# One scale in place of five for the value matrices of five batches, and a new order table

## The chip, the cores and the metric

The kernel runs on one core of a Trainium2 chip. The metric is the device time of one execution in microseconds (us). The names used are those of the profile: PE is the matmul engine and PEld its weight loads, DVE, ACT and POOL are the vector, scalar and GpSimd engines, SP is the engine that issues nearly all DMAs (SPq its queue).

## The reference

Attention for 8 batches of 8 heads (sequence 576, head size 64) with a bias that depends on positions alone, then a gated layer on the heads put side by side (512 columns).

```python
scores = scale * np.matmul(q, k.transpose(0, 1, 3, 2))
...
scores = scores + bias.transpose(2, 0, 1)[None, :, :, :]
scores = scores - np.max(scores, axis=-1, keepdims=True)
attn = np.exp(scores)
attn = attn / (np.sum(attn, axis=-1, keepdims=True) + 1e-09)
return np.matmul(attn, v).astype(np.float32)
...
for k in range(K):
    gate_pre += conv_w[k][None, None, :] * xp[:, k:k + S, :]
gate = 1.0 / (1.0 + np.exp(-gate_pre))
val = x @ w_val
return (gate * val @ w_out).astype(np.float32)
```

## The kernel before

The work is cut into 32 pairs of heads (`order`: first batches 0 and 1, then batch after batch from 2 to 7, four pairs each, numbered 0 to 31) and 8 gated layers (`mlp`). A pair computes four blocks of 128 query rows, and every second pair a shared fifth block with the last 64 rows of two pairs. Per block: PE multiplies q and k into the PSUM tile `t_sp` (L702), DVE adds the bias and finds the row's extreme (`logits`, L748), ACT takes the exponential (`expo`, L760).

`TRANS` then has two ways. In the way "T" (pairs 0 to 5, 24 and 25) PE transposes the weights in fp32 (L891). In the way "D" (the other 24 pairs) ACT, DVE or POOL rounds the exponentials to fp16 (`top`, L195), POOL or DVE forms the rest (`rest`, L218), and a DMA on SP's queue transposes both parts (`swap`, L925 and L928). For the product with the values (`piece`, L958) the values of a D pair are split in two fp16 parts as well. That split is what the change is about:

- `ldv` (L630, L618 in the way T) loads a pair's values, 128 x 640 numbers, into `raw`, a buffer of the ring `w` that has 13; `vmax` (L633) finds the greatest magnitude of each partition on DVE and puts it in `vcol`.
- `vp_mm` (L636) transposes that column on PE, `vp_max` (L640) takes the greatest of all on DVE, `vscale` (L644) makes the pair's scale of it, `vinv` (L650) the inverse. These four steps run for each D pair.
- `vhi` (L654, ACT) writes the first fp16 part with the inverse as factor, `vlo` (L657, DVE) the second; from here on `piece` may run.
- PE's product is brought to SBUF (`t_xp`, the gated layer's input) by ACT with the pair's scale as factor (`ev`, `evr`, L213) and multiplied with the softmax' inverse sums by DVE (`mu`, L1014).

A batch has a scale of its own for the gated layer's input (`batch_scale`): `vb_max` (L570), `vb_mm` (PE, L573), `vb_all` (L576), `vb_scale`, `vb_inv` (L582). It is used much later, when ACT and DVE split `t_xp` in two fp16 parts: `split_hi` (L213, out `xh`), `split_lo` (L206, out `xl`). On POOL `split_lo` takes four instructions by way of `gtmp`. The gate is a convolution on `t_xp` (`taps`, L1151) and a Tanh on ACT (`sig`, L1164).

No queue decides the order at run time. `ORDER` is a packed table: for each place the number of a task and the engine that it goes to, of those that the task allows. Each engine runs its instructions in that order, and an instruction that has to wait holds up all behind it on its engine. A ring's buffer goes to its next taker in the table's order.

## Time and profile before

| | us |
|---|---|
| three runs, median (lowest to highest) | 663.69 (659.8 to 665.06) |
| profiled execution, its own time | 663.0 |
| its span, first to last instruction | 661.2 |
| PE, DVE, ACT, POOL busy in the span | 626.6, 596.0, 573.5, 489.2 |
| granted TensorE clock, mean | 0.988 |

The span is 1.8 us shorter than the execution's own time, which is 0.7 us under the median of the three runs. A busy time counts an instruction from its start to its end; on one engine the start of the next often lies before the end of the one ahead, and the profile's sums leave out what overlaps.

### The profile page before, as it was taken

The page shows a single profiled execution, that of the slowest core. Times are in us where ns is not written, and L with a number is a line of the kernel's source. Part 1 is how long each engine was busy: PE and PEld are TensorE (multiplying, and loading weights), DVE is VectorE, ACT ScalarE, POOL GpSimd, SP SyncE. Part 2 cuts the span into 40 slices and gives each one's busy share as a digit, 9 for nine tenths or more (in the row PEclk, how much of TensorE's full clock was granted, in tenths as well). Part 3 has the DMA queues.
Part 4 walks back from the last instruction along what each step waited for, and adds up shares of the span by engine and source line. Part 5 has one row for each costly group of instructions (what it writes and reads, how often), then busy time and mean ns, then how long its engine had stood idle before and what let it go on. Part 6 is the DMA issues. An engine that isn't in the chain of part 4 may idle for free.

```text
span 661.2 us, 16769 instructions
## 1 busy us (share of the span) xinstructions
PE 626.6 (95%) x6176; PEld 405.1 (61%) x6176; DVE 596.0 (90%) x1604; ACT 573.5 (87%) x1268; POOL 489.2 (74%) x539
## 2 busy tenths in 40 slices
PE   6869999999799999999998999999999999999997
PEld 2213667766466677657665576666676765767663
DVE  7999999999999799899998888998988889989982
ACT  6989999999899999889787999889889878989671
POOL 5576739676699898897788788887868868776430
PEclk9969999999999999999999999999999999999999
DMA  5879966336999999999999999999984998999622
GB/s 178 270 254 326 333 242 182 103 140 145 170 209 190 207 218 211 234 192 216 204 209 234 212 208 206 224 184 208 217 179 120 161 210 178 219 196 162 120 80 95
DMA packets 279106, 129.76 MB, mean 196 GB/s; under 512 B 255600, under 2 KB 255856, under 8 KB 279024
## 3 DMA queue, kind: packets, MB, share of 16 engines
q1 hardware_dynamic: 278880, 128.40, 89.5%
q8 instruction: 48, 0.79, 0.5%
q14 instruction: 34, 0.28, 0.2%
q10 hardware_dynamic: 144, 0.29, 0.1%
HBM read 44.64 MB, written 20.33 MB: 98 GB/s over the span
## 4 chain that ended last, share of the span: by engine, by line
PE 52%; DVE 13%; DMA 13%; POOL 9%; ACT 9%; issue 3%; SPq 1%; DVEq 0%; POOLq 0%; ACTq 0%
PE t_sp L702 12%; DMA t_pt<-t_d 12%; PE t_ps L958 10%; PE t_ps L1285 8%; PE t_ps L1219 7%; POOL t_d L218 6%; PE t_ps L891 5%; DVE t_d L748 4%; PE t_ps L337 4%; ACT t_d L760 3%; ACT t_d L195 2%; PE t_sp L718 2%; DVE rel L318 2%; PE t_ps L1004 1%; PE t_ps L1028 1%
## 5 line engine op out<-in xcount | busy, mean ns | idle before, releaser
L218 POOL TENSOR_TENSOR t_d<-t_d,t_d 128x128 f16<-128x128 f32 (+1 forms) x180 | 244.3, 1376 | 50.9 <-ACT t_d L195 46.5
L760 ACT ACTIVATE t_d<-t_d,nm 128x576 f32<-128x576 f32 x288 | 221.5, 771 | 24.3 <-DVE nm L748 23.6
L748 DVE CUSTOM_DVE_ANT_0 t_d<-t_sp,bias 128x576 f32<-128x576 f32 x256 | 186.4, 750 | 22.8 <-PE t_sp L702 16.4
L702 PE MATMUL t_sp<-t_qk 64*128 64x288 f32 x1024 | 170.0, 431 | 4.8 <-DVE nm L748 3.7
L958 PE MATMUL t_ps<-t_pt,t_w 128*64 128x256 f16 (+1 forms) x1664 | 122.6, 296 | 7.3 <-DMA t_pt<-t_d 4.1
L702 PEld LDWEIGHTS t_sp<-t_qk 64*128 64x128 f32 x1024 | 96.1, 187 | 52.6 <-DVE nm L748 16.2
L195 ACT CAST t_d<-t_d 128x576 f16<-128x576 f32 x155 | 99.6, 666 | 12.2 <-DMA t_pt<-t_d 7.6
L1219 PEld LDWEIGHTS <-wv 128*128 128x128 f16 x768 | 72.6, 98 | 29.6 <-issue 10.3
L958 PEld LDWEIGHTS <-t_w 128*64 128x64 f16 x1344 | 70.3, 110 | 24.6 <-issue 15.6
L1219 PE MATMUL t_ps<-xh,wv 128*128 128x256 f16 (+1 forms) x480 | 68.3, 286 | 0.0
L1151 DVE SCALAR_TENSOR_TENSOR t_ps<-t_xp,convw,t_ps 128x288 f32<-128x288 f32 x126 | 64.5, 516 | 1.6 <-ACT t_ps L1142 0.4
L1285 PE MATMUL t_ps<-wo,gh 128*128 128x512 f16 x240 | 57.8, 380 | 0.0
L760 ACT ACTIVATION_READ_ACCUMULATOR t_d<-t_d,nm 128x1 f32 x288 | 54.9, 191 | 0.0
L337 PE MATMUL t_ps<-rel,w 128*32 128x280 f32 (+17 forms) x352 | 44.5, 555 | 9.6 <-ACT t_be L356 4.4
L318 POOL TENSOR_SCALAR rel<-gt,sct,nb 128x560 f32<-128x560 f32 (+11 forms) x16 | 37.4, 2341 | 18.1 <-PE t_ps L337 17.8
L810 POOL TENSOR_SCALAR t_d<-t_d,rinv 128x576 f32<-128x576 f32 x56 | 41.9, 761 | 8.6 <-DVE rinv L790 7.6
L318 DVE TENSOR_SCALAR rel<-gt,sct,nb 128x576 f32<-128x576 f32 (+17 forms) x92 | 46.9, 570 | 1.2 <-PE t_ps L337 1.0
L891 PE MATMUL t_ps<-ident,t_d 128*128 128x128 f32 x324 | 43.4, 278 | 1.9 <-POOL t_d L810 0.8
L891 PEld LDWEIGHTS t_ps<-ident,t_d 128*128 128x128 f32 x324 | 35.3, 140 | 14.1 <-issue 4.4
L199 POOL TENSOR_SCALAR t_d<-t_d 128x576 f16<-128x576 f32 x47 | 34.0, 727 | 12.8 <-ACT t_d L760 10.5
L1285 PEld LDWEIGHTS <-gh 128*128 128x128 f16 x240 | 22.3, 99 | 27.4 <-issue 6.0
L195 ACT COPY t_pt<-t_ps 128x512 f32<-128x512 f32 (+1 forms) x82 | 36.2, 489 | 3.2 <-PE t_ps L891 2.8
(149 smaller groups left out, 1081.8 us busy)
## 6 DMA issues: line engine op xcount, KB each, us to landing
t_qk<-qkd SPq DMA_DIRECT2D x32, 576.0 KB, 4.7
bias_d<-t_be SPq DMA_DIRECT2D x36, 295.5 KB, 4.2
bias<-bias_d SPq DMA_DIRECT2D x16, 576.0 KB, 7.2
out<-t_w SPq DMA_DIRECT2D x32, 256.0 KB, 2.6
t_w<-vd SPq DMA_DIRECT2D x24, 320.0 KB, 3.7
t_w<-vn SPq DMA_DIRECT2D x8, 320.0 KB, 4.4
t_d<-wvd SPq DMA_DIRECT2D x4, 512.0 KB, 4.9
t_d<-wod SPq DMA_DIRECT2D x4, 512.0 KB, 4.1
```

Source lines behind the costliest of these rows:

```text
L195: A.copy(out=out, in_=in_)
L218: (V if e == "V" else G).tensor_tensor(out=out, in0=in0, in1=in1, op=ALU.subtract)
L318: (G if e == "G" else V).tensor_scalar(out=rel[g].t[:, 0:w], in0=src, scalar1=sct[:, mm : mm + 1], scalar2=nb1, op0=ALU.mult, op1=ALU.max,)
L337: T.matmul(pb[32 * g : 32 * g + 32, 0 : y - x], lhsT=w28, rhs=rel[g].t[:, x:y], start=True, stop=True, tile_position=(0, 32 * g),)
L702: T.matmul(ts[a][:, j, 0:hw], lhsT=qk.t[r, c * P : (c + 1) * P], rhs=qk.t[r, x : x + hw], start=True, stop=True,)
L748: V.tensor_tensor_reduce(out=part(c, a).rearrange("p (j f) -> p j f", j=2), in0=sp.t[:, :, 0 : S // 2], in1=bias.rearrange("p (j f) -> p j ...
L760: A.activation(out=part(c, a), in_=part(c, a), func=AF.Exp, bias=nms[c][:, a : a + 1], scale=-1.0, accum_out=sums[c][:, a, 0:1],)
L891: T.transpose(t[:, k * P : (k + 1) * P], es[c].t[:, (k0 + k) * P : (k0 + k + 1) * P], ident)
L958: T.matmul(po.t[r, 0:256], lhsT=vt.t[:, v, r], rhs=pt[:, x, :, :] if tr else pt[:, :, x, :], start=(t == 0 and m == 0), stop=(t == 4 and m ...
L1151: V.scalar_tensor_tensor(out=o, in0=x, scalar=wt, in1=t, op0=ALU.mult, op1=ALU.add)
L1219: T.matmul(pm.t[:, 0:w], lhsT=weights["wv"][wi][:, k, d * P : (d + 1) * P], rhs=xb.t[xi][:, k, 0:w], start=(q == 0 and k == 0), stop=(q == ...
L1285: T.matmul(pm.t, lhsT=gb.t[gi][:, k, o : o + P] if o < 256 else gx.t[gi][:, k, :], rhs=weights["wo"][wi][:, k, :], start=(q == 0 and k == ...
```

## The change

`WHOLE` names batches 2 to 6. For them the first pair of a batch makes the tasks that load the values of all four pairs and find their maxima (`value`), and then the batch's scale, which now also serves the values of all four. The steps `vp_mm`, `vp_max`, `vscale` and `vinv` are gone for the 18 D pairs of these batches (16 of batches 2 to 5, two of batch 6) and stay for the six others. `vhi` and `vlo` wait for `vb_inv` of the batch. `t_xp` holds the values divided by a power of two times that scale, so `ev` and `evr` take a constant as factor, `split_hi` a plain copy and `split_lo` a plain subtraction; the gate's Tanh takes a factor from memory, `vb_scale` has a second instruction, and the two T pairs of batch 6 take a factor where they had a plain copy. Line numbers of the changed kernel are higher (L636 is L651, L633 is L615).

```diff
@@ -45,37 +45,36 @@
 ORDER = (
-    'c-l=^0ca}unfJXnnn^MylQ<@0GD*fbNycQ7Op-}5N#;G=!-9LbhYwtEi+i|-JzQ`X-
...
+    'c-nPW0cbMmnKu7Fnn^MylQ<@mWRgtGBpH)QoFrp1N#;N7VT&!c_#f`!7Pq*E2QJvdJ
...
 )
@@ -84,6 +83,8 @@
+VTOP = 2.0**12
+WHOLE = range(2, B - 1)
@@ -223,8 +224,7 @@
-    bsc = cp.tile([P, B, 4], F32, name="bsc")
-    gtmp = cp.tile([P, 320], F32, name="gtmp")
+    bsc = cp.tile([P, B, 5], F32, name="bsc")
@@ -576,11 +576,16 @@
         def vb_scale(e):
-            scalars(e, bsc[:, b, 2:3], bsc[:, b, 1:2], 1e-30, 1.0 / TOP, ALU.max)
+            scalars(e, bsc[:, b, 2:3], bsc[:, b, 1:2], 1e-30, 1.0 / (VTOP if b in WHOLE else TOP), ALU.max)
+            if b in WHOLE:
+                scalars(e, bsc[:, b, 1:2], bsc[:, b, 2:3], VTOP / TOP, 0.5)
 
         def vb_inv(e):
             V.reciprocal(out=bsc[:, b, 3:4], in_=bsc[:, b, 2:3])
-
+            if b in WHOLE and any(TRANS[n // 2] for n in range(len(order)) if order[n][1] == b):
+                scalars("V", bsc[:, b, 4:5], bsc[:, b, 3:4], TOP / VTOP, 1.0)
+
+        plan.at = ("batch", b)
         t = add([("V", 0.1)], vb_max, maxima[b], s0 + 1)
         t = add([("P", 0.14)], vb_mm, [t], s0 + 1.5, [tb])
         t = add([("V", 0.2)], vb_all, [t], s0 + 2, (), [tb])
@@ -591,6 +596,28 @@
+    values = {}
+
+    def value(n):
+        hg, b, l = order[n]
+        p = 2 * hg + l
+        s0 = PER * n + PAIR_AT[n]
+        plan.at = ("pair", n)
+        vt = Buf("vt")
+        raw = vt if TRANS[n // 2] else Buf("raw")
+
+        def ldv(e):
+            new(raw, [P, 5, P], F32)
+            SP.dma_start(raw.t.rearrange("p t d -> p (t d)"), (vn if raw is vt else vd)[b, p])
+
+        def vmax(e):
+            V.tensor_reduce(out=vcol[:, b, p : p + 1], in_=raw.t, op=ALU.max, axis=AX.XY, apply_absolute_value=True)
+
+        t0 = add([("S", 0.9)], ldv, (), s0 - 1, [raw])
+        t1 = add([("V", 0.74)], vmax, [t0], s0 - 0.5, (), [raw])
+        maxima.setdefault(b, []).append(t1)
+        return vt, raw, t0, t1
@@ -609,28 +636,16 @@
-        vt = Buf("vt")
+        vt, raw, tv, t1 = values.pop(n) if n in values else value(n)
         sc = {}
-        if tr:
-
...
-        else:
-            raw, tb = Buf("raw"), Buf("tt")
...
+        if b in WHOLE and b not in scaled_by:
+            for k in range(n + 1, len(order)):
+                if order[k][1] == b:
+                    values[k] = value(k)
+            batch_scale(b, s0)
+            plan.at = ("pair", n)
+        if not tr:
+            tb = Buf("tt")
 
             def vp_mm(e):
                 T.transpose(bank(tb)[:, 0:P], vcol[:, b, p : p + 1].to_broadcast([P, P]), ident)
@@ -649,28 +664,31 @@
+            def vinv_():
+                return bsc[:, b, 3:4] if b in WHOLE else sc["t"][:, 2:3]
+
             def vhi(e):
                 new(vt, [P, 10, P], F16)
-                A.activation(out=vt.t[:, 0:5, :], in_=raw.t, func=AF.Copy, scale=sc["t"][:, 2:3])
+                A.activation(out=vt.t[:, 0:5, :], in_=raw.t, func=AF.Copy, scale=vinv_())
...
-                    scalar=sc["t"][:, 2:3],
+                    scalar=vinv_(),
...
             d = s0 - 1
-            t0 = add([("S", 0.9)], ldv, (), d - 1, [raw])
-            t1 = add([("V", 0.74)], vmax, [t0], d)
-            maxima.setdefault(b, []).append(t1)
-            t2 = add([("P", 0.14)], vp_mm, [t1], d + 0.2, [tb])
-            t2 = add([("V", 0.2)], vp_max, [t2], d + 0.3, (), [tb])
-            t2 = vscaled = add(SMALL, vscale, [t2], d + 0.5)
-            t2 = add([("V", 0.08)], vinv, [t2], d + 0.6)
+            if b in WHOLE:
+                t2, vscaled = scaled_by[b], None
+            else:
+                t2 = add([("P", 0.14)], vp_mm, [t1], d + 0.2, [tb])
+                t2 = add([("V", 0.2)], vp_max, [t2], d + 0.3, (), [tb])
+                t2 = vscaled = add(SMALL, vscale, [t2], d + 0.5)
+                t2 = add([("V", 0.08)], vinv, [t2], d + 0.6)
             t3 = add([("A", 0.73)], vhi, [t2], d + 1, [vt])
             tv = add([("V", 0.8)], vlo, [t3], d + 1.5, (), [raw])
@@ -681,6 +699,15 @@
+        def put(e, out, in_, sc):
+            if not tr:
+                scaled_copy(e, out, in_, TOP / VTOP if b in WHOLE else sc["t"][:, 1:2])
+            elif b in WHOLE:
+                scaled_copy(e, out, in_, bsc[:, b, 4:5])
+            else:
+                copy(e, out, in_)
@@ -938,8 +965,9 @@
         xo = arrived[b]
-        if len(maxima[b]) == NP:
+        if len(maxima[b]) == NP and b not in scaled_by:
             batch_scale(b, s0)
+            plan.at = ("pair", n)
@@ -978,16 +1006,13 @@
                     V.memset(xo.t[:, :, 0:4], 0.0)
-                if tr:
-                    copy(e, xo_(g * 256, (g + 1) * 256), po.t[:, 0:256])
-                else:
-                    scaled_copy(e, xo_(g * 256, (g + 1) * 256), po.t[:, 0:256], sc["t"][:, 1:2])
+                put(e, xo_(g * 256, (g + 1) * 256), po.t[:, 0:256], sc)
...
-                [last, x1] + ([] if tr else [vscaled]) + ([taker.get(b)] if g == 0 else []),
+                [last, x1, scaled_by.get(b) if tr else vscaled] + ([taker.get(b)] if g == 0 else []),
@@ -1043,10 +1068,7 @@
             def evr(e):
-                if tr:
-                    copy(e, me["xo"](512, S), por.t[:, 0:D])
-                else:
-                    scaled_copy(e, me["xo"](512, S), por.t[:, 0:D], me["sc"]["t"][:, 1:2])
+                put(e, me["xo"](512, S), por.t[:, 0:D], me["sc"])
@@ -1078,8 +1100,9 @@
         def oscale(e):
-            scalars(e, bsc[:, b, 0:1], bsc[:, b, 2:3], wsc[:, 4:5], 1.0)
-            scalars(e, oscx[odd_at, b_pair : b_pair + 1], bsc[odd_at, b, 2:3], wsc[odd_at, 4:5], 1.0)
+            up = VTOP / TOP if b in WHOLE else 1.0
+            scalars(e, bsc[:, b, 0:1], bsc[:, b, 2:3], wsc[:, 4:5], up)
+            scalars(e, oscx[odd_at, b_pair : b_pair + 1], bsc[odd_at, b, 2:3], wsc[odd_at, 4:5], up)
@@ -1161,7 +1184,7 @@
         def sig(e, ks):
             for k in ks:
-                A.activation(out=gates[k].t, in_=gates[k].t, func=AF.Tanh, scale=0.5)
+                A.activation(out=gates[k].t, in_=gates[k].t, func=AF.Tanh, scale=bsc[:, b, 1:2] if b in WHOLE else 0.5)
@@ -1182,16 +1205,17 @@
                     x = xp.t[:, k : k + 2, 4 + t0 : 4 + t0 + w]
-                    scaled_copy(e, xb.t[0][:, k : k + 2, 0:w], x, bsc[:, b, 3:4])
+                    if b in WHOLE:
+                        copy(e, xb.t[0][:, k : k + 2, 0:w], x)
+                    else:
+                        scaled_copy(e, xb.t[0][:, k : k + 2, 0:w], x, bsc[:, b, 3:4])
 
                 def split_lo(e, k=k, t0=t0, w=w, xb=xb):
                     x, h, l = xp.t[:, k : k + 2, 4 + t0 : 4 + t0 + w], xb.t[0][:, k : k + 2, 0:w], xb.t[1][:, k : k + 2, 0:w]
-                    if e == "V":
+                    if b in WHOLE:
+                        sub(e, l, x, h)
+                    else:
                         scaled(e, l, x, bsc[:, b, 3:4], h, ALU.subtract)
-                        return
-                    for y in range(2):
-                        scalars(e, gtmp[:, 0:w], x[:, y], bsc[:, b, 3:4], 1.0)
-                        sub(e, l[:, y], gtmp[:, 0:w], h[:, y])
@@ -1203,7 +1227,8 @@
-                u = add([("V", 0.72 + 1.2 * x1), ("G", 2.4 + 4 * x1)], split_lo, [h], base + 0.3 * k + 0.5, (), [xp])
+                us = [("V", 0.72 + 1.2 * x1)] + ([("G", 0.8 + 1.8 * x1)] if b in WHOLE else [])
+                u = add(us, split_lo, [h], base + 0.3 * k + 0.5, (), [xp])
```

The table is another one, but its tasks stand nearly as they stood: of 3842 tasks that both have by name, 28 go to another engine, and 24 stand more than 20 places from where they stood among these. Three places show what it does.

PE, batch 2, ahead of an output matmul of the gated layer (L1285, L1310 in the changed kernel), before and after. `t_sp` are scores, `vcol` the column of maxima:

```order
L1004 MATMUL t_ps_153<-ident,rinvs 64x128 x4
L702 MATMUL t_sp_427<-t_qk_186 128x288
L702 MATMUL t_sp_428<-t_qk_186 128x288
L702 MATMUL t_sp_427<-t_qk_186 128x288
L702 MATMUL t_sp_428<-t_qk_186 128x288
L636 MATMUL t_ps_205<-ident,vcol 128x128
L1285 LDWEIGHTS gh
L1285 MATMUL t_ps_193<-wo_104,gh 128x512
```

```order
L1029 MATMUL t_ps_192<-ident,rinvs 64x128 x4
L729 MATMUL t_sp_426<-t_qk_185 128x288
L729 MATMUL t_sp_427<-t_qk_185 128x288
L729 MATMUL t_sp_426<-t_qk_185 128x288
L729 MATMUL t_sp_427<-t_qk_185 128x288
L1310 LDWEIGHTS gh
L1310 MATMUL t_ps_180<-wo_103,gh 128x512
```

The transpose of a pair's maxima is gone, and its neighbours follow on one another.

DVE, batch 4, from `vmax` of pair 17 on, before (buffer numbers kept) and after:

```order
L633 TENSOR_REDUCE vcol_94<-t_w5_250 128x1
L1229 SCALAR_TENSOR_TENSOR t_w12_479<-t_w9_258,t_ps0_153 128x320
L1053 TENSOR_TENSOR t_xp_3539<-t_xp_3539,t_ps1_181 128x64
L748 ISA t_d4_710,nm_4512<-t_sp0_427,biasr_93 128x576
L748 ISA nm_4512 128x1
L748 ISA t_d4_710,nm_4512<-t_sp1_428,biasr_93 128x576
L748 ISA nm_4512 128x1
L202 TENSOR_SCALAR bsc_95<-bsc_95,wsc_101 128x1
L202 TENSOR_SCALAR oscx_97<-bsc_95,wsc_101 64x1
L640 TENSOR_REDUCE vsc_4519<-t_ps2_193 128x1
L644 TENSOR_SCALAR vsc_4519<-vsc_4519 128x1
L650 RECIPROCAL vsc_4519<-vsc_4519 128x1
```

```order
L615 TENSOR_REDUCE vcol_94<-t_w0_163 128x1
L570 TENSOR_REDUCE bsc_95<-vcol_94 128x1
L1075 TENSOR_TENSOR t_xp_3512<-t_xp_3512,t_ps1_180 128x64
L576 TENSOR_REDUCE bsc_95<-t_ps2_192 128x1
L203 TENSOR_SCALAR bsc_95<-bsc_95 128x1 x2
L584 RECIPROCAL bsc_95<-bsc_95 128x1
L775 ISA t_d4_709,nm_4469<-t_sp0_426,biasr_93 128x576
L775 ISA nm_4469 128x1
```

Before, the pair's own scale (L640, L644, L650) stands nine rows behind the maximum. After, the batch's scale (L570, L576, L203, L584) stands right behind the last of the four maxima with one row between, and L576 needs a transpose that PE makes of L570's result.

SP, batch 5, the loads from `vd` (L630; L612 in the changed kernel) among the transposes (L925, L952), before and after:

```order
L925 DMA_TRANSPOSE t_pt0_896<-t_d4_710 128x18x128
L609 DMA t_qk0_186<-qkd 128x1152
L925 DMA_TRANSPOSE t_pt1_942<-t_d3_590 128x18x128
L925 DMA_TRANSPOSE t_pt0_896<-t_d0_163 128x18x128
L925 DMA_TRANSPOSE t_pt1_942<-t_d5_824 128x18x128
L1303 DMA out<-t_w10_327 128x512
L925 DMA_TRANSPOSE t_pt0_896<-t_d3_590 128x18x128
L609 DMA t_qk1_210<-qkd 128x1152
L630 DMA t_w3_198<-vd 128x640
L1303 DMA out<-t_w5_250 128x512
```

```order
L952 DMA_TRANSPOSE t_pt1_941<-t_d6_848 128x18x128
L952 DMA_TRANSPOSE t_pt0_895<-t_d4_709 128x18x128
L612 DMA t_w1_164<-vd 128x640
L636 DMA t_qk0_185<-qkd 128x1152
L1328 DMA out<-t_w7_255 128x512
L952 DMA_TRANSPOSE t_pt1_941<-t_d3_589 128x18x128
L952 DMA_TRANSPOSE t_pt0_895<-t_d6_848 128x18x128
L952 DMA_TRANSPOSE t_pt1_941<-t_d0_162 128x18x128
L952 DMA_TRANSPOSE t_pt0_895<-t_d3_589 128x18x128
L636 DMA t_qk1_203<-qkd 128x1152
L1328 DMA out<-t_w4_248 128x512
```

The load of pair 23's values stood behind four transposes, two loads of q and k and a store of the output, and now stands ahead of them.

## Rows read from the trace of the kernel before

**Rows 1.** The page's first part: busy us (share of the span) xinstructions.

```profile
PE 626.6 (95%) x6176; PEld 405.1 (61%) x6176; DVE 596.0 (90%) x1604; ACT 573.5 (87%) x1268; POOL 489.2 (74%) x539
```

**Rows 2.** Busy us (xinstructions) by stretch: PE, PEld, DVE, ACT, POOL, clock, DMA, GB/s.

```profile
0.00:180.00 180.00, 159.35 (x1338) 91.53 (x1338) 169.98 (x463) 164.45 (x378) 118.87 (x139) 0.96 0.71 213
180.00:370.00 190.00, 184.52 (x1937) 124.13 (x1938) 176.52 (x472) 170.82 (x373) 160.97 (x172) 1.00 1.10 212
370.00:550.00 180.00, 176.02 (x1849) 119.47 (x1847) 159.95 (x451) 159.02 (x353) 146.82 (x158) 1.00 1.00 194
550.00:640.00 90.00, 89.34 (x966) 61.12 (x966) 82.10 (x201) 75.25 (x157) 59.55 (x68) 1.00 0.84 161
```

**Rows 3.** The chain that ended last, by engine.

```profile
PE 52%; DVE 13%; DMA 13%; POOL 9%; ACT 9%; issue 3%; SPq 1%; DVEq 0%; POOLq 0%; ACTq 0%
```

**Rows 4.** Instructions by form, scale steps: xcount | busy us, mean ns | idle before.

```profile
L636 PE MATMUL t_ps<-ident,vcol 128*128 128x128 f32 x24 | 7.0, 300 | 0.1
L640 DVE TENSOR_REDUCE vsc<-t_ps 128x1 f32<-128x128 f32 x24 | 6.7, 281 | 1.0 <-PE t_ps L636 0.8
L644 DVE TENSOR_SCALAR vsc<-vsc 128x1 f32<-128x1 f32 x18 | 2.6, 145 | 0.1
L650 DVE RECIPROCAL vsc<-vsc 128x1 f32<-128x1 f32 x24 | 3.7, 155 | 0.1
```

**Rows 5.** Timeline of PE at two transposes of maxima: start us, us, what.

```profile
207.59 0.32 PE L636 MATMUL t_ps<-ident,vcol 128*128 128x128 f32 x1
207.75 2.75 PE L1285 MATMUL t_ps<-wo,gh 128*128 128x512 f16 x12
...
415.11 0.27 PE L636 MATMUL t_ps<-ident,vcol 128*128 128x128 f32 x1
415.21 0.71 PE L1219 MATMUL t_ps<-xh,wv 128*128 128x320 f16 x4
```

**Rows 6.** Timeline of DVE at two scale steps.

```profile
345.82 0.29 DVE L640 TENSOR_REDUCE vsc<-t_ps 128x1 f32<-128x128 f32 x1
346.03 0.81 DVE L633 TENSOR_REDUCE vcol<-t_w 128x1 f32<-128x640 f32 x1
...
353.08 0.15 DVE L644 TENSOR_SCALAR vsc<-vsc 128x1 f32<-128x1 f32 x1
353.15 0.75 DVE L748 CUSTOM_DVE_ANT_0 t_d<-t_sp,bias 128x576 f32<-128x576 f32 x1
```

**Rows 7.** Pieces of the chain, in order of time: start us, us, what.

```profile
148.10 0.40 DVE vsc L640 x2
...
526.10 0.08 DVE vsc L650
```

**Rows 8.** Instructions by form on ACT, factor from memory and without.

```profile
L213 ACT ACTIVATE t_xp<-t_ps,vsc 128x256 f32<-128x256 f32 x48 | 22.0, 462 | 2.5 <-PE t_ps L1004 2.0 <-PE t_ps L958 0.4
L195 ACT COPY t_xp<-t_ps 128x256 f32<-128x256 f32 x11 | 4.0, 364 | 0.0
L1111 ACT ACTIVATE t_w<-t_xp,convw 128x576 f32<-128x576 f32 x28 | 21.1, 766 | 0.5 <-DVE t_xp L1053 0.4
L1164 ACT ACTIVATE t_w<-t_w 128x576 f32<-128x576 f32 x32 | 21.4, 674 | 2.5 <-POOL t_w L1116 1.1 <-DVE t_w L1116 1.0 <-DVE t_w L1151 0.5
```

**Rows 9.** Instructions by form on DVE, the two kinds of subtraction.

```profile
L206 DVE SCALAR_TENSOR_TENSOR xl<-t_xp,bsc,xh 128x640 f16<-128x640 f32 x14 | 12.9, 937 | 0.0
L218 DVE TENSOR_TENSOR t_d<-t_d,t_d 128x1024 f16<-128x1024 f32 x17 | 22.8, 1344 | 0.4
```

**Rows 10.** Waits of SP's queue: us in total, times, longest us.

```profile
SPq L630 <- POOL t_w L1116: 8.9, 2, 8.0
```

**Rows 11.** Timeline of SP's queue ahead of pair 23's load of values.

```profile
410.03 9.21 SPq L925 DMA_TRANSPOSE t_pt<-t_d  x3
424.96 0.33 SPq L630 DMA_DIRECT2D t_w<-vd  x1
```

**Rows 12.** Waits of DVE for PE: us in total, times, longest us.

```profile
DVE t_d L748 <- PE t_sp L702: 16.4, 31, 2.2
DVE vsc L640 <- PE t_ps L636: 0.8, 1, 0.8
```

73 lines of the change are left out of this document (30 added, 43 removed).

## The prediction

> **What bounds the kernel now.** I read the page's first part, then the stretches, then the chain. PE is busy for 95% of the span, DVE 90%, ACT 87% [rows 1]. In the stretches the reader is to see where PE is not: 20.6 us of its 34.6 idle us lie before 180 us, where the bias is made, 3.9 at the very end, and between 180 and 640 us, where the 18 pairs of the change run, only 10.1 of 460 [rows 2]: 5.5, 4.0 and 0.7 us in the three stretches. The chain is not PE's alone: PE holds 52% of it, DVE and DMA 13% each, POOL and ACT 9% each [rows 3]. So PE's stream sets most of the pace, and each of the others some of it. A busy PE is not a PE at its peak, since its instructions overlap; what an instruction costs PE is read from starts, not from durations.
>
> **The change part by part.** First PE. The 18 transposes of maxima go. One lasts 300 ns in the mean [rows 4], but the matmul behind it starts 0.16 us after it in one place (207.59 to 207.75) and 0.10 in another (415.11 to 415.21) [rows 5]; over the 24 the median of that distance, without idle time, is 0.16. I take 18 x 0.16 = 2.9 us; the ends are 18 x 0.10 = 1.8 and, by whole durations, 18 x 0.30 = 5.4. The five transposes for the batches stay.
>
> DVE loses 18 maxima over the transposed column (281 ns), 13 of the small products (145 ns; the other five were POOL's) and 18 inverses (155 ns) [rows 4]: 5.1 + 1.9 + 2.8 = 9.8 us by durations. By starts one maximum costs 0.21 us (345.82 to 346.03) and one product 0.07 (353.08 to 353.15) [rows 6], the inverse as little as the product: 18 x 0.21 + 31 x 0.07 = 6.0 us. The added small instructions (a second one in each batch's scale and one more in batch 6, and four products come to DVE from POOL or anew) take back some 7 x 0.07 = 0.5 us. `split_lo` gains nearly nothing on DVE: the product with subtraction takes 937 ns for 640 elements, the plain subtraction 1344 ns for 1024 [rows 9], which is 1.46 and 1.31 ns an element, a gain of up to 0.1 us in each of 18, 1.8 us at most and I take 0.9. Much of this lies beside PE's work and is worth nothing there.
>
> ACT: a factor from memory costs time. The eviction of 256 columns takes 462 ns with it and 364 without, and 576 columns 766 ns (a product) against 674 (the Tanh with its constant) [rows 8]. So the 54 evictions of the 18 pairs save 54 x 0.1 = 5.4 us, 17 parts of `xh` on ACT 1.7 us, and 20 Tanh pay 20 x 0.09 = 1.8: 5.3 us of ACT in sum. Two more casts of 576 columns go to ACT. ACT's share of the chain is 9%, so some 0.5 us of that is on the path. POOL's change is small either way: two `split_lo` of four instructions each become two of one.
>
> What of all this lay on the path? In the chain itself I find ten pieces of the steps that go, from half of the 0.40 us at 148.10 to 0.08 us at 526.10 [rows 7], 1.3 us in sum. That is the first-order gain: what is left if the work behind is late for other reasons at once. PE's stream gives 2.9 when PE is the pace-setter. I take PE's 2.9 and for ACT and DVE 0.6: **3.5 us**, with 1.3 and 6.0 (DVE's stream) as ends.
>
> Then what is added as a wait. `vhi` of a batch's first pair now waits for all four loads and maxima. In the table this costs no place: the four loads were early before too, and for all pairs but pair 8 `vhi` stands within some ten places of where it stood. For pair 8 it comes some 90 places later, and `vlo` ends 4 places ahead of the first product (95 before), which has to wait for the pair's DMA transposes anyway. Behind a late `vlo` everything on PE waits. The batch's scale is a trip from DVE to PE and back with one row of cover on DVE (batch 4): DVE stands in L576 until PE has come to the transpose. The near row is the same trip before: DVE waited once for L636 in 24, 0.8 us [rows 12]; the far one is DVE's longest wait for a score matmul, 2.2 us. Five trips cost between 0 and 11 us; I take the near row, once, on DVE, which PE's queue of waiting work hides.
>
> The moved load of pair 23: it needs a buffer of the ring `w` in front of four transposes. SP is full there, with three transposes in 9.21 us [rows 11]. A load from `vd` has waited 8.0 us for its buffer once, and next to nothing in the other cases [rows 10]. Cost between 0 and 8 us; I take 0.
>
> The 28 tasks on other engines and the few moved ones have no price of their own in the trace; they are small and go both ways, and I put them into the range.
>
> Sum: 663.0 for the profiled execution, less 3.5, is **659.5 us**, or 0.6% under the median of the three runs, 663.69. A measurement of this kernel tells about 1% from no change (the three runs lie 5.3 us apart).
>
> **The rivals.** DVE sets the pace. It is at 90% [rows 1], and its share of work that goes is the greatest: 6.0 - 0.5 + 0.9 = 6.4 us by starts, so 656.6 us. For it: PE's idle time inside the stretches and DVE's and ACT's 22% of the chain [rows 3]. Against it: in the two middle stretches PE is idle for 9.5 us and DVE for 33.5 [rows 2], so DVE waits more than PE does. The Trainium skill (Perfetto Trace Analysis, Identifying the Most-Contended Engine) says that matmul busy time misleads for TensorE, where the busy share of weight loads is to be taken, and that occupancy is a fair measure for the others. By that rule PE stands at the 61% of its weight loads and DVE with its 90% is the bound, and with DVE's durations the time would be 663.0 - 9.8 = 653.2. The trace agrees on the overlap of matmuls (rows 5), but not on the order of the two: the chain gives PE four times DVE's share.
>
> Nothing of it arrives: transposes by DMA and POOL's subtractions, which lose no work, end last again as soon as PE and DVE are earlier; they hold 22% of the chain. Then the gain is about the first-order 1.3 us or less: 662.
>
> Slower: pair 23's load finds its buffer taken. If it waits for the 8.0 us of rows 10, four transposes behind it are that much later, PE's products of those pairs with them, and the time is 663.0 - 3.5 + 8.0 = 667.5 us. It is slower than before from 3.5 us of wait on. For it: SP is in order, and the load now asks for its buffer 20 us earlier than at 424.96. Against it: one such wait among the 24.
>
> **How the numbers follow.** Forecast 659.5: 0.50. DVE's pace, 656.6: 0.22. Nothing arrives, 662: 0.16. Slower, 667.5: 0.12. Faster by over 1% is under 657.1: half of the second case, and the forecast's own tail with larger effects of the moved tasks, 0.17: 0.28. Slower by over 1% is over 670.3: the part of the last case in which two places wait, 0.08. The same: 0.64. The range goes from 652, where DVE's durations would put it, to 667.5.
>
> **What would show it.** In the profile of the changed kernel PE's busy time should be some 3 to 5 us lower at an unchanged idle time of about 10 us between 180 and 640; 6 of the transposes of maxima should be left; evictions should take about 364 ns; DVE should lose about 8 to 10 us of busy time and gain as much idle time. If the load in front of the four transposes waits for microseconds in SP's waits, the slower rival holds. If PE's busy time falls by 5 us and PE's idle time grows by as much, nothing arrived. It is wrong if the new order has moved a stall that I don't see from names alone: a bias phase with other idle times, or a fall of the granted clock, would show in the first stretch.

## The result and the profile after

The changed kernel is slower. Over 20 executions of each, on one chip, it takes 666.02 us in the median (661.3 to 670.52), the kernel before 662.61 (658.77 to 665.08). The ratio is 1.0052 with a 95% interval of 1.0035 to 1.0069: 3.4 us more, where 3.5 us less (from 663.0) was forecast. The time lies inside the range on record (652.0 to 667.5) and inside the 1% that was called "the same", but on the other side of the kernel before, beyond the measurement's uncertainty. The profiled execution took 668.18 us, 2.2 us more than the kernel's median. Ratios here and below leave disturbed executions out, so that a ratio need not be that of the two medians beside it.

The page's first part, of the changed kernel:

```profile
PE 624.5 (94%) x6158; PEld 403.4 (61%) x6158; DVE 587.5 (88%) x1552; ACT 569.8 (86%) x1274; POOL 482.5 (72%) x531
```

All four engines have less to do than in [rows 1]: PE 2.1 us, DVE 8.5, ACT 3.7, POOL 6.7. The work did go. The forms of the steps that were to go or to get cheaper (count, then busy us and mean ns):

```profile
L651 PE MATMUL t_ps<-ident,vcol 128*128 128x128 f32 x6 | 1.7, 290 | 0.0
L214 ACT ACTIVATE t_xp<-t_ps 128x256 f32<-128x256 f32 x36 | 13.3, 374 | 4.2 <-PE t_ps L1029 3.5 <-PE t_ps L986 0.7
L1187 ACT ACTIVATE t_w<-t_w,bsc 128x576 f32<-128x576 f32 x20 | 15.2, 766 | 0.6 <-DVE t_w L1174 0.3
```

Six transposes of maxima are left of 24 [rows 4]; an eviction takes 374 ns in place of 462, a Tanh with its factor from memory 766 [rows 8]. The stretches say where the time went (columns as in [rows 2]):

```profile
0.00:180.00 180.00, 157.61 (x1353) 90.79 (x1355) 170.17 (x463) 166.09 (x383) 120.70 (x140) 0.97 0.71 215
180.00:370.00 190.00, 181.47 (x1883) 121.45 (x1880) 168.91 (x436) 162.14 (x360) 153.08 (x161) 0.98 1.07 206
370.00:550.00 180.00, 173.70 (x1818) 117.47 (x1816) 156.20 (x430) 158.51 (x358) 142.72 (x153) 1.00 0.96 191
550.00:640.00 90.00, 89.26 (x979) 60.66 (x977) 80.67 (x203) 74.40 (x158) 59.34 (x70) 1.00 0.91 175
```

Between 180 and 640 us PE stands idle for 8.5 + 6.3 + 0.7 = 15.6 us, where [rows 2] had 10.1, and from 180 to 370 its mean clock is no longer 1.00. Before which of PE's instructions the idle time lies is told by the groups of this window, here the products of probabilities and values, first of the kernel before, then of the changed one (after the last bar: idle time ahead of the group, and what ended it):

```profile
L958 PE MATMUL t_ps<-t_pt,t_w 128*64 128x256 f16 (+1 forms) x1390 | 90.7, 280 | 6.9 <-DMA t_pt<-t_d 4.1 <-DVE t_xp L1014 2.0 <-DVE vsc L640 0.4
```

```profile
L986 PE MATMUL t_ps<-t_pt,t_w 128*64 128x256 f16 (+1 forms) x1382 | 91.1, 282 | 10.9 <-DMA t_pt<-t_d 5.6 <-DVE t_ps L1174 2.0 <-DVE t_xp L1039 1.7
```

6.9 us have become 10.9: PE comes to a product whose transposed probabilities are still on their way through a DMA (1.5 us more), or in front of which DVE still works on a PSUM tile (L1174, 2.0 us). Another 1.2 us end with the second part of the values (`vlo`, L675). Three of PE's pauses after 60 us are longer than the longest there of the kernel before, 1.54 us: 2.04, 2.03 and 1.96 us. PE's timeline of the changed kernel around the first two:

```profile
316.51 1.24 PE L729 MATMUL t_sp<-t_qk 64*128 64x288 f32 x8
319.79 2.08 PE L986 MATMUL t_ps<-t_pt,t_w 128*64 128x256 f16 x28 [2.04 <-DVE t_ps L1174]
321.60 1.12 PE L1029 MATMUL t_ps<-ident,rinvs 128*64 128x128 f32 x8
322.65 2.09 PE L729 MATMUL t_sp<-t_qk 64*128 64x288 f32 x8
...
348.52 0.32 PE L573 MATMUL t_ps<-ident,bsc 128*128 128x128 f32 x1
350.87 2.42 PE L986 MATMUL t_ps<-t_pt,t_w 128*64 128x256 f16 x28 [2.03 <-DMA t_pt<-t_d]
353.22 2.17 PE L729 MATMUL t_sp<-t_qk 64*128 64x288 f32 x8
```

Eight score matmuls last 1.24 us ahead of the first pause and 2.09 and 2.17 us after the two. The stretches of 2 us show why (third figure from the end: the granted clock):

```profile
318.00:320.00 2.00, 0.21 (x4) 0.24 (x6) 2.00 (x7) 0.26 (x1) 0.47 (x2) 1.00 1.24 267
320.00:322.00 2.00, 2.00 (x32) 2.00 (x30) 0.49 (x2) 1.18 (x3) 1.92 (x2) 0.75 1.11 204
322.00:324.00 2.00, 2.00 (x14) 1.39 (x12) 0.00 (x0) 1.24 (x4) 1.92 (x4) 0.50 1.16 221
324.00:326.00 2.00, 2.00 (x14) 1.10 (x13) 1.22 (x4) 1.03 (x2) 0.20 (x1) 0.90 0.56 90
```

Behind the pause the clock is at 0.50, its lower level of 1.2 GHz, for 3.4 us (half of the stretch with 0.75, all of the next, a fifth of the one with 0.90). The kernel before shows no such stretch between 56 and 650 us.

Each pair of heads has nine exponentials on ACT. Set side by side by the start of every ninth, the changed kernel is ahead by some 1.3 us at nearly all of them up to 315 us of the kernel before, then behind by 1.5 at 333, 4.8 at 367, 6.4 at 424 and 7.1 at 473 us, and ends 5.1 us late in span. So the loss comes in four steps of 2 to 3 us between pairs 15 and 24, with a part won back between them.

### The profile page after: what moved, and what is told of

Its sections match the earlier page's. It is cut to its first block, busy times and chain, and to the rows that moved or that the text cites. A ratio compares the mean times of both kernels' runs of the same rounds, so it can differ in the third digit from the quotient of the medians.

```text
span 666.3 us, 16688 instructions
## 1 busy us (share of the span) xinstructions
PE 624.5 (94%) x6158; PEld 403.4 (61%) x6158; DVE 587.5 (88%) x1552; ACT 569.8 (86%) x1274; POOL 482.5 (72%) x531
## 4 chain that ended last, share of the span: by engine, by line
PE 50%; ACT 17%; DMA 14%; DVE 9%; POOL 6%; issue 3%; SPq 1%; ACTq 0%; DVEq 0%; POOLq 0%
DMA t_pt<-t_d 12%; PE t_sp L729 12%; PE t_ps L986 11%; PE t_ps L1244 8%; PE t_ps L1310 8%; ACT t_d L787 6%; PE t_ps L918 5%; POOL t_d L219 4%; ACT t_d L196 3%; DVE t_d L775 3%; DVE rel L318 2%; ACT t_be L356 2%; PE t_sp L745 2%; PE t_ps L1029 1%; PE t_ps L337 1%
## 5 line engine op out<-in xcount | busy, mean ns | idle before, releaser
L219 POOL TENSOR_TENSOR t_d<-t_d,t_d 128x1024 f16<-128x1024 f32 (+1 forms) x180 | 243.3, 1370 | 58.1 <-ACT t_d L196 53.7
L986 PE MATMUL t_ps<-t_pt,t_w 128*64 128x256 f16 (+1 forms) x1664 | 124.0, 297 | 11.5 <-DMA t_pt<-t_d 5.6
L196 ACT CAST t_d<-t_d 128x576 f16<-128x576 f32 x157 | 100.9, 667 | 15.6 <-DMA t_pt<-t_d 10.1
L1174 DVE SCALAR_TENSOR_TENSOR t_ps<-t_xp,convw,t_ps 128x288 f32<-128x288 f32 x126 | 64.6, 518 | 1.6 <-ACT t_ps L1165 0.3
L1310 PE MATMUL t_ps<-wo,gh 128*128 128x512 f16 x240 | 58.0, 380 | 0.0
L337 PE MATMUL t_ps<-rel,w 128*32 128x280 f32 (+17 forms) x352 | 41.8, 559 | 11.9 <-ACT t_be L356 7.5
L318 DVE TENSOR_SCALAR rel<-gt,sct,nb 128x544 f32<-128x544 f32 (+17 forms) x92 | 46.8, 569 | 1.5 <-PE t_ps L337 1.3
L219 POOL TENSOR_TENSOR gl<-t_w,gh 128x256 f16<-128x256 f32 x43 | 32.7, 761 | 9.0 <-ACT gh L196 5.5
```

What stands on the lines that cost most here:

```text
L196: A.copy(out=out, in_=in_)
L219: (V if e == "V" else G).tensor_tensor(out=out, in0=in0, in1=in1, op=ALU.subtract)
L318: (G if e == "G" else V).tensor_scalar(out=rel[g].t[:, 0:w], in0=src, scalar1=sct[:, mm : mm + 1], scalar2=nb1, op0=ALU.mult, op1=ALU.max,)
L337: T.matmul(pb[32 * g : 32 * g + 32, 0 : y - x], lhsT=w28, rhs=rel[g].t[:, x:y], start=True, stop=True, tile_position=(0, 32 * g),)
L986: T.matmul(po.t[r, 0:256], lhsT=vt.t[:, v, r], rhs=pt[:, x, :, :] if tr else pt[:, :, x, :], start=(t == 0 and m == 0), stop=(t == 4 and m ...
L1174: V.scalar_tensor_tensor(out=o, in0=x, scalar=wt, in1=t, op0=ALU.mult, op1=ALU.add)
```

## The experiments

Times are medians; the ratio, with its 95% interval, is to the kernel before on the same chip, whose medians lay between 661.4 and 663.2 us.

| run | us | ratio |
|---|---|---|
| the changed kernel | 666.02 | 1.0052 (1.0035 to 1.0069) |
| old_order | 673.19 | 1.0157 (1.0119 to 1.0196) |
| new_order | 671.14 | 1.0127 (1.0097 to 1.0157) |
| fill_two | 665.02 | 1.0056 (1.0034 to 1.0078) |
| add18 | 667.48 | 1.0082 (1.0052 to 1.0112) |
| fixed_scale | 659.76 | 0.9966 (0.9943 to 0.9990) |
| batch5_own | 666.21 | 1.0059 (1.0031 to 1.0088) |
| batch5_fill | 664.04 | 1.0034 (1.0013 to 1.0056) |
| load23_early | 667.39 | 1.0081 (1.0050 to 1.0111) |
| no_wait | 666.07 | 1.0074 (1.0045 to 1.0103) |
| old_nowait | 674.37 | 1.0188 (1.0142 to 1.0234) |
| whole34 | 664.61 | 1.0028 (1.0002 to 1.0055) |
| old_free | 658.38 | 0.9919 (0.9889 to 0.9949) |
| new_late | 662.85 | 0.9994 (0.9971 to 1.0016) |
| new_back | 659.58 | 0.9962 (0.9939 to 0.9985) |
| before_bias_fill | 665.86 | 1.0002 (0.9965 to 1.0039) |
| after_bias_fill | 664.28 | 1.0029 (1.0001 to 1.0058) |

The first theory (A) was that the two pauses and the clock behind them are the loss; the rivals were the searched table (B) and the wait for the batch's scale (C).

**old_order.** The changed code, with the table of the kernel before in which only forced things move.

```diff
 ORDER = (
-the changed kernel's places and engines
+the places and engines of before; scales of batches 2 to 6, vhi and vlo of pair 8 where the changed kernel has them
+the loads and maxima that these need: just ahead of them, where they stood later
```

> The changed kernel's arithmetic (one scale for a batch) in the order and on the engines of the kernel before; only what the arithmetic forces is moved: the batches' scales, vhi and vlo of pair 8, and a few loads and maxima by some places. Theory A (pauses and clock: what leaves PE is given back where PE waits for a DMA transpose, and a pause of some 2 us there is followed by about 4 us at half clock, as at 319.8 and 350.9 us of the changed kernel's trace): no better than the changed kernel, 664 to 667 us, with pauses of 2 us in front of products and stretches of granted clock 0.5 behind them. Theory B (the searched table: its new places and engines cost the time, the arithmetic itself gains): 659 to 661 us, as forecast, below the kernel before. Theory C (a wait for the batch's scale holds a late vlo): as slow as the changed kernel, with PE waiting for vlo (the product with subtraction on DVE) and not for a DMA transpose.

673.19 us: slower than both kernels, and by more than any of the three theories said. With the order of before, the new dependence costs 11 us; the new table wins 7 of them back. B in the form "the arithmetic gains and the table loses" falls for a table that has the early scales in it. The trace shows where PE waits now; these are its waits from 180 to 640 us (us in total, times, longest; L566 is the transpose for a batch's maximum, L979 a product):

```profile
PE t_ps L979 <- DMA t_pt<-t_d: 6.4, 5, 3.1
PE t_ps L566 <- ACT t_w L1127: 2.9, 1, 2.9
PE t_sp L722 <- DVE nm L768: 2.3, 3, 1.8
PE t_ps L566 <- DVE bsc L563: 1.9, 1, 1.9
```

PE stands in front of the batch's transpose, and everything in its queue behind it stands too: 7.2 us in all. Only 1.9 of them end with the batch's maximum (L563); 1.3 and 1.0 end with an instruction of DVE that reads a PSUM tile (L1247, L1167) and 2.9 with one of ACT. So beside the late maximum, a PSUM bank that is not free yet when the transpose comes early is a rival reason, and no run tells the two apart. The chain at one of these places, batch 5, begins with the load of pair 23 that the batch's maximum needs:

```profile
417.93 3.15 DMA t_w<-vd
421.08 0.02 issue
421.10 0.83 DVE vcol L608
421.93 0.02 issue
421.95 0.17 DVE bsc L563
422.12 0.04 issue
422.17 0.32 PE t_ps L566
```

**new_order.** The code of before, with the changed kernel's places and engines.

```diff
 ORDER = (
-the places and engines of before
+the changed kernel's; the 18 pairs' own maxima, transposes, products and inverses behind their old neighbours
```

> The kernel before, with its pair scales and all 18 transposes, in the order and on the engines of the changed kernel; the pairs' own maxima stand behind the neighbours that they had before. Theory A: within 1 us of the kernel before, 662 to 664 us, since the transposes stand in the pauses again and no pause reaches 2 us. Theory B: slower than before by what the changed kernel lost or more, 666 to 670 us. Theory C: 662 to 664 us as well, so this run tells only A and C from B.

671.14 us, just above the range that B gave. With old_order as bad, either table with the other kernel's arithmetic costs 8 to 10 us. But both tables have the early scales in them: in this run too PE's transposes for batches 2 to 6 stand at 200, 268, 353, 419 and 508 us, as in the changed kernel, although the arithmetic of before needs their result only later. So the two runs don't show that a table fits its own arithmetic alone. The run old_free, below, has the changed arithmetic in the old table without early scales, and is the fastest of all.

**fill_two.** Work for PE in the two pauses.

```diff
+FILL = {(15, 2): 10, (17, 4): 10}
...
+        def fill(c, ts):
+            for _ in range(FILL.get((n, c), 0)):
+                T.transpose(ts[1][:, 1, 384:512], ident, ident)
```

> The changed kernel with ten transposes of the identity, into columns that nobody reads, behind each of two score groups: the ones after which PE pauses for 2.04 us (at 317.75) and 2.03 us (at 348.85) in the changed kernel's trace. Theory A: PE has work in these pauses, the granted clock stays at 1.00 behind them, and the time falls by 2 to 4 us, to 662 to 664 us, although 20 instructions are added. Theory B and C: the pauses are only symptoms, the clock is not what costs, and the time is that of the changed kernel or up to 3 us above it, 666 to 669 us.

In the profiled execution both places do what A said. PE's timeline of this run at the first (L720 is the filler, L993 the product):

```profile
315.41 1.24 PE L734 MATMUL t_sp<-t_qk 64*128 64x288 f32 x8
316.58 1.31 PE L720 MATMUL t_sp<-ident 128*128 128x128 f32 x10
317.91 1.72 PE L993 MATMUL t_ps<-t_pt,t_w 128*64 128x256 f16 x28
319.43 0.63 PE L1036 MATMUL t_ps<-ident,rinvs 128*64 128x128 f32 x8
319.99 1.24 PE L734 MATMUL t_sp<-t_qk 64*128 64x288 f32 x8
```

No pause, no fall, score groups of 1.24 us. But the median is 665.02, and the ratio that of the changed kernel (1.0056 against 1.0052): A gave 662 to 664. With these two pauses filled another, of 2.24 us, stands at 419.48 us in this execution, and no fall of the clock follows it.

**add18.** The transposes of the pairs' maxima back on PE, read by nobody.

```diff
             if b in WHOLE:
                 t2, vscaled = scaled_by[b], None
+                add([("P", 0.14)], vp_mm, [t1], d + 0.2, [tb], [tb])
```

> The changed kernel with the 18 transposes of the pairs' maxima put back on PE, each beside its old neighbour on PE; nobody reads their result, and the 18 maxima, products and inverses on DVE stay out. Theory A: the transposes fill part of the pauses, fewer pauses reach 2 us, and the time is at or under that of the changed kernel, 663 to 666 us. Theory B and C: they cost up to their 2.9 us, 666 to 669 us.

667.48 us, inside the range of B and C, and not under the changed kernel. The removed transposes were no useful filling. A is not the main cause.

The next four price the work that goes by itself, and look at the place where one load was moved far: pair 23's, which the changed kernel issues ahead of three transposes, together with a load of scores' inputs and a store. SP's timeline of the changed kernel there:

```profile
412.59 0.57 SPq L612 DMA_DIRECT2D t_w<-vd  x1
413.25 0.39 SPq L636 DMA_DIRECT2D t_qk<-qkd  x1
413.74 0.38 SPq L1328 DMA_DIRECT2D out<-t_w  x1
414.21 11.37 SPq L952 DMA_TRANSPOSE t_pt<-t_d  x3
```

The three transposes hold SP for 11.37 us, in [rows 11] 9.21, and the first lands 7.13 us after its start.

**fixed_scale.** The kernel before, without the 18 chains.

```diff
+VFIX, FIXED = 2.0**9, range(2, B - 1)
...
-                A.activation(out=vt.t[:, 0:5, :], in_=raw.t, func=AF.Copy, scale=sc["t"][:, 2:3])
+                A.activation(out=vt.t[:, 0:5, :], in_=raw.t, func=AF.Copy, scale=VFIX if b in FIXED else sc["t"][:, 2:3])
...
-            t2 = add([("P", 0.14)], vp_mm, [t1], d + 0.2, [tb])
+            if b not in FIXED:
+                t2 = add([("P", 0.14)], vp_mm, [t1], d + 0.2, [tb])
```

> The kernel before, in its own order and on its own engines, in which the 18 pairs of batches 2 to 6 take a constant of 512 as scale: the 18 transposes, maxima, products and inverses are gone as in the changed kernel, the evictions take a constant, and nothing waits for a batch's maximum (no scale is measured, that is what is left out). It prices the work that the change takes away, without what it adds. The forecast's step (PE's 2.9 us and 0.6 of ACT and DVE arrive): 658 to 660 us, 3 us under the kernel before. Theory N (nothing arrives: PE comes earlier to products that wait for a DMA transpose, and a pause there may bring a fall of the clock): 661 to 665 us, not under the kernel before by more than 1 us, with longer pauses in front of products.

659.76 us, ratio 0.9966: near the forecast's 659.5, reached by leaving work out and adding nothing. Theory N ("nothing arrives") allowed 1 us; the gain is 2.3, with an interval of 0.7 to 3.8, so this run speaks against it and only old_free, below, rules it out. It speaks against A too: the profiled execution has a pause of 3.12 us ahead of a product at 306.0 us and 6.8 us of half clock, loses 4.3 us between the starts of pairs 14 and 15, and has won 3.4 of them back by the start of pair 24. So the gain exists, and what the change adds takes it back and 3.4 us more.

**batch5_own.** Batch 5 with a scale for each pair again, and its transfers moved back.

```diff
-WHOLE = range(2, B - 1)
+WHOLE = (2, 3, 4, 6)
```

> The changed kernel with the arithmetic of before for batch 5 alone: pairs 20 to 23 have their own scales again, so that pair 20's split no longer waits for pair 23's load; that load, its maximum and the first store of batch 3 go back behind the transposes of pairs 19 and 20 on SP, all else keeps its place. Theory D (the early load is the price of the shared scale: load, store and scores' inputs stand ahead of three transposes, and PE loses some 2.8 us between 406 and 424 us): 663 to 664 us, 2 to 3 us under the changed kernel, and the loss between the starts of pairs 20 and 21 is gone. Rival (any change to a searched order costs, whatever it undoes, as putting one kernel's arithmetic in the other's order did): 667 to 671 us.

666.21 us: no gain, where theory D gave 663 to 664. Between the starts of pairs 20 and 21 the profiled execution still loses 1.7 us against before, in the changed kernel 2.8. **batch5_fill** adds the fillers of fill_two to it (the same diff as there):

> The kernel with batch 5's own scales, and the ten transposes of the identity behind each of the same two score groups as in the run fill_two. If the pauses with their clock falls and the early load are what the changed kernel lost, and they add: 660 to 663 us, at or under the kernel before. If they don't add, or any change costs: 665 us or more.

664.04 us, between the two answers: 2 us less than batch5_own, which is within the uncertainty of the two, and still over the kernel before. **load23_early** moves the one load:

```diff
-place 2483 of the table: load of values, pair 23
+place 2439, behind a swap of pair 18: load of values, pair 23
```

> The changed kernel with pair 23's load moved forward on SP by five transposes, to right behind the load of pair 22's values and a swap of pair 18: it is no longer among the transfers right ahead of the three transposes. Theory D in its narrow form (this one transfer right ahead of the transposes costs): 664 to 665 us, with the loss between the starts of pairs 20 and 21 1 to 2 us smaller. In its wide form (the load costs wherever it stands between transposes, since these fill SP and the DMA engines from 200 to 480 us): 666 to 668 us, with the same loss some 20 us earlier.

667.39 us, in the range of D's wide form, but its loss between the starts of pairs 20 and 21 is no smaller (from 3.1 to 7.4 us behind) and stands where it stood: this load is not the cause by itself.

**no_wait.** The changed kernel's table, with constants where the batch's scale was read; every instruction is still there.

```diff
+VMOST = 0.5
...
-            scalars(e, bsc[:, b, 2:3], bsc[:, b, 1:2], 1e-30, 1.0 / (VTOP if b in WHOLE else TOP), ALU.max)
+            scalars(e, bsc[:, b, 2:3], bsc[:, b, 1:2], VMOST if b in WHOLE else 1e-30, 1.0 / (VTOP if b in WHOLE else TOP), ALU.max)
...
-                return bsc[:, b, 3:4] if b in WHOLE else sc["t"][:, 2:3]
+                return VTOP / VMOST if b in WHOLE else sc["t"][:, 2:3]
...
-                scaled_copy(e, out, in_, bsc[:, b, 4:5])
+                scaled_copy(e, out, in_, TOP / VMOST)
```

> The changed kernel, in its own order and on its own engines, with every instruction of it, but the values of batches 2 to 6 are split by a constant (8192), which the batch's scale then is as well (its floor stands above the largest value), so that no split and no eviction waits for a batch's maximum; that the scale follows the data is what is left out. Theory W (the wait for the batch's scale costs what the changed kernel lost): 660 to 662 us, as the run with fixed scales in the old order. Theory O (the wait itself is short, and what costs is the order that was given for it: loads and stores ahead of transposes, later splits): 664 to 667 us, as the changed kernel.

666.07 us, as the changed kernel. The splits' wait is not what costs: theory W (and C) falls, O stands. **old_nowait** has the same diff on old_order:

> The run old_order (the changed kernel's arithmetic in the order of the kernel before, with the forced moves) with the same constant in place of the batch's scale, so that nothing waits for it. Theory W: 660 to 662 us, since the order is that of before and no wait is left; so of old_order's 11 us over the kernel before all is wait. Theory O: 668 to 673 us, since the early loads and the transposes for the batches' maxima stand where they stood in old_order.

674.37 us: O again. Also without any split that waits, the old order with the forced moves is 12 us slower than before; the transposes for the batches' maxima are still in PE's queue. **whole34** asks whether two batches without far moves keep their gain:

```diff
-WHOLE = range(2, B - 1)
+WHOLE = (3, 4)
 ORDER = (
-the changed kernel's places and engines
+the places and engines of before; the two batches' scales where the changed kernel has them
```

> The kernel before's order with the shared scale for batches 3 and 4 alone (eight of the 18 pairs); batches 2, 5 and 6 keep a scale for each pair, and no load has to move far. If the cost of the shared scale comes from the places where a load or a split had to move (pair 8, pair 23, batch 6), these two batches keep their part of the gain: 8/18 of 2.5 us, so 660.5 to 662 us, at or a little under the kernel before. If each batch costs: 664 us or more.

664.61 us, ratio 1.0028: each batch costs, also where no load has to move far.

What of the order costs, the last three of this line tell, each undoing one thing more than no_wait; the prices hold for this order of undoing. The scale is a constant in them; in addition one group of Tanh of batch 6 reads its factor before the late chain has written it. **new_late** puts the five chains (maximum, transpose, maximum, scale, inverse) back behind their batches, 25 tasks in all (two of the scales go to POOL again with it), **new_back** also the moved transfers and splits, and **old_free** has the changed arithmetic in the order of before.

```diff
-                t2, vscaled = scaled_by[b], None
+                t2, vscaled = t1, None
...
-                [last, x1, scaled_by.get(b) if tr else vscaled] + ([taker.get(b)] if g == 0 else []),
+                [last, x1, None if tr else vscaled] + ([taker.get(b)] if g == 0 else []),
 ORDER = (
-no_wait: the scale of batch 2 at place 1252, of 3 at 1649, of 4 at 2132, of 5 at 2526, of 6 at 3065
+new_late: at 1464, 2049, 2280, 2912, 3510
...
-new_late: load of pair 23 at 2483, first store of batch 3 at 2523, split of pair 8 at 1263 and 1267
+new_back: at 2579, 2560, 1170 and 1179, and four others likewise
...
-new_back: 21 tasks on other engines than before, some 900 moved, most by one or two places
+old_free: none
```

> The changed kernel's arithmetic with the constant 8192 as scale, in the order and on the engines of the kernel before with nothing forced: the batches' maxima, transposes and scales stand late, where they stood before (that the scale follows the data is left out). If the rest of the changed arithmetic (Tanh with a factor from memory, plain subtractions, the second product in a batch's scale) costs nothing: 659 to 661 us, as fixed_scale. If it costs: above 662 us.

> The run no_wait (the changed kernel's order and engines, constant scale) with the chains for the scales of batches 2 to 6 put back to where they stood in the kernel before, behind the batch; loads and stores stay as the changed kernel has them. Theory P (PE's queue stands behind the batch's transpose, which waits for the last load of the batch): 660 to 662 us. Theory L (loads and stores ahead of transposes cost) and theory S (the table's other engines and small moves cost): 664 to 667 us, as no_wait.

> As new_late, and the moved transfers and splits too are put back beside their old neighbours: the loads of pairs 16 and 23, the maxima of pairs 10 and 23, the first store of batch 3, pair 25's scores' inputs, and pair 8's split. What is left of the changed order are its 22 other engines and its many moves by a few places. Theory P or L: 660 to 662 us. Theory S: 664 to 667 us.

658.38, 662.85 and 659.58 us. Theory P is borne out in the main by new_late (0.9994 after 1.0074, though 662.85 lies between the two answers), L by new_back in a smaller part that is no larger than its uncertainty, S by what is left between new_back and old_free. The old order says the same of the early chains, more loudly: old_nowait differs from old_free by the same 25 tasks and 16 others that had to move with them, and by 2.7%, 17.8 us (some 3.6 either way), although no split waits in either. What an early chain costs depends on the order around it; in the changed kernel's searched table the step from no_wait to new_back, which undoes nearly the same, is 7.4 us. PE's idle time from 180 to 640 us goes the same way, one profiled execution each: 15.5 us in no_wait, 11.8 in new_late, 10.9 in new_back, 8.1 in old_free. The group of the products of old_free:

```profile
L980 PE MATMUL t_ps<-t_pt,t_w 128*64 128x256 f16 (+1 forms) x1390 | 91.6, 283 | 6.7 <-DMA t_pt<-t_d 5.3 <-DVE t_xp L1033 1.3
```

**before_bias_fill and after_bias_fill** ask whether a fall of the clock costs by itself: transposes of the identity ahead of the pauses in the bias.

```diff
+BFILL = {(19, 0): 6, (16, 0): 14, (23, 0): 12}
...
+            for _ in range(BFILL.get((m, j), 0)):
+                T.transpose(standing["sp", 0][:, 896:1024], ident, ident)
```

> The kernel before with 32 transposes of the identity, into columns that nobody reads, behind three of the bias's matmul groups: 6, 14 and 12 of them, ahead of the pauses at 32.18, 33.94 and 42.25 us of its trace. After the last two the granted clock falls to 0.50 and PE works 5.97 and some 5 us without a gap at it. If the clock costs time by itself: the falls at 34 to 42 and 45 to 52 us are gone or shorter, and the time falls by 2 to 5 us, to 657 to 660 us. If the bias stretch is set by ACT and DVE (18.7 and 19.2 us busy of 20) or if what is won there is lost at the next wait: 661 to 664 us, no change.

> The same 32 transposes in the changed kernel, behind the same groups (its pauses there are 1.14, 1.89 and 2.00 us). If the clock costs time by itself: 2 to 5 us under the changed kernel, 661 to 664 us. If not: 665 to 667 us.

The falls in the bias are gone in both. From 34 to 52 us the stretch of before_bias_fill, whose mean clock was 0.62 in the kernel before:

```profile
34.00:52.00 18.00, 13.07 (x130) 5.85 (x124) 17.90 (x40) 16.74 (x36) 13.62 (x7) 1.00 0.86 278
```

The bias gains a little by it: in the kernel before, DVE was busy for 16.86 of these 18 us, here for 17.90, and from the second pair on the exponentials start 1.2 us earlier. The time doesn't follow: 1.0002 (and a wide spread, 658 to 671 us) and 1.0029. In the profiled execution of before_bias_fill a fall that the kernel before doesn't have, from 177.7 us and 6.8 us long, takes the 1.2 us back. So for the kernel before the expectation's rival holds, that what is won in the bias is lost behind it; for the changed kernel the gain (0.2%) is no larger than the uncertainty.

## Why the prediction was wrong

**The work that goes** was sized well. 3.5 us were forecast; fixed_scale gives 0.34% (2.3 us, interval 0.7 to 3.8), old_free, with the rest of the changed arithmetic, 0.81% (5.4 us, 3.4 to 7.3). "Nothing of it arrives" gave a gain of 1.3 us or less and falls with old_free. DVE as the pace-setter gave 6.4 us, which old_free's interval does not exclude; against it stands that DVE did not pass on all that it lost: in old_free's profiled execution it is busy for 586.8 us, 9.2 less than before, in a span 3.5 us shorter (657.7), and in the changed kernel for 8.5 us less in a longer one. The rule of the Trainium skill (Perfetto Trace Analysis, Identifying the Most-Contended Engine), by which DVE was the bound, led to the estimate of 653.2, which no run reached; in this case's trace DVE's idle time between 180 and 640 us rose from 41 to 54 us, and the time rose with it.

**The step that failed** is "Then what is added as a wait": "Five trips cost between 0 and 11 us; I take the near row, once, on DVE, which PE's queue of waiting work hides". It was put at nothing. The runs show 0.80% between no_wait and new_late, 5.3 us (adding the two intervals by squares, some 2.5 either way): inside the bounds of 0 to 11, not at their end. The wait was also seen from one side only. DVE does wait for PE's transpose, for 1.4 us at three of the five chains of the changed kernel; but PE waits in front of DVE's maximum as well, and with it all that stands behind the transpose in its queue. The waits of the batch's transpose in the changed kernel (weight load and matmul together), all eight batches:

```profile
L573 PE MATMUL t_ps<-ident,bsc x8: 272/322/323, 89.6 to 611.8; 128*128 128x128 f32 x8
its engine sat idle before it (us, times) until:
  DVE bsc L570: 3.7, 6
...
who waited for it (us, times):
  DVE bsc L576: 1.4, 3
```

In the kernel before nothing waits ahead of this transpose for L570, because the table has it hundreds of places later, when the maximum is long there. Only 1.1 us of the 3.7 is idle time of the matmuls themselves. Of the rest of the 5.3 us, a part is seen as later transposes by DMA and longer pauses in front of products, here no_wait and then new_late:

```profile
L987 PE MATMUL t_ps<-t_pt,t_w 128*64 128x256 f16 (+1 forms) x1368 | 90.4, 283 | 12.2 <-DMA t_pt<-t_d 10.0 <-DVE t_w L676 1.3 <-DVE t_xp L1040 0.7
L980 PE MATMUL t_ps<-t_pt,t_w 128*64 128x256 f16 (+1 forms) x1390 | 92.9, 285 | 9.5 <-DMA t_pt<-t_d 6.0 <-DVE t_xp L1033 1.6 <-DVE nm L769 1.5
```

Through which instruction it gets there was not shown, nor whether the late maximum or the PSUM bank that the transpose takes earlier is the reason. "In the table this costs no place" was read from the splits, which do stand where they stood; the chain itself had moved up by 150 to 450 places, and that was not priced.

**The moved load of pair 23**, "between 0 and 8 us; I take 0": the slower rival's mechanism was wrong. The load is issued 12.4 us earlier than before (not 20) and doesn't wait for a buffer. The waits of SP's queue in the changed kernel have one such row, and it is that of [rows 10] again, of a later load: it ends at 510.06 us, before at 503.49:

```profile
SPq L612 <- POOL t_w L1139: 8.3, 1, 8.3
```

All moved transfers and splits together cost 0.32%, 2.1 us (about as much either way, so the size is open); the load by itself could not be shown to cost anything, neither where batch 5 gave it up nor where it was moved forward.

**The 28 tasks on other engines and the small moves** "go both ways" and stood in the range alone. (Counted by tasks, new_back has 21 on other engines than old_free.) With everything else undone they cost 0.43%, 2.8 us (some 2.5 either way).

The sum: -5.4 + 2.8 + 2.1 + 5.3 = 4.8 us. It has to come to the 4.9 of no_wait (0.74%), since the terms are differences between that run and the kernel before; the changed kernel itself is at 3.4 (0.52%), within the uncertainty. The sizes come from runs on several chips, each against the kernel before on its own. The true slower case, then, is not one stall but an order that fits less well at many places, and a rival of that form was not among those on record.

**What was to show it.** PE's busy time fell by 2.1 us in place of 3 to 5, with time at half clock inside it; its idle time between 180 and 640 us rose by 5.5, where none was expected; both were named as signs against the forecast. DVE's 8 to 10 us were right. The fall of the granted clock was named for the first stretch; it came in the second. How much it costs stays open: over 63 executions of six kernels, within each kernel, one microsecond more of lost clock (span times one less the mean clock) goes with 0.60 us of time (0.2 either way), and the changed kernel loses 8.2 us of clock in the mean, the kernel before 6.1. If the one caused the other, that would be a share of some 1.3 us; fill_two and the bias runs show that taking falls away needn't give time back.

No version that takes its scale from the data beat the kernel before: after_bias_fill (1.0029) came closest among those with the shared scale in all five batches, whole34 (1.0028) among all. Those that did beat it leave the data's scale out.

## What to carry to other kernels

Price a shared quantity by where its last input comes in each queue, not by the instructions that it saves: five reductions over four pairs each, moved up in in-order queues, cost 5.3 us here although no split waited for their result. Where the order was searched, split an edit in three (the work alone in the old order, the new waits in the new order, the new order alone) before believing a sum; here the work alone gave the forecast's number and the order took it back. A local repair that works in one execution, such as filling a pause, has to be read from the median.
